# Batch 2 loaded apart from q, batch 1 in two steps, and the output's copies, PSUM buffers and DMAs regrouped

## The chip, the cores and the metric

One core of a Trainium2 chip. Its engines are TensorE (PE; PEld are its weight loads), VectorE (DVE), ScalarE (ACT), GpSimd (POOL) and SyncE (SP), which issues every DMA of this kernel. Each engine runs its own instructions in the order in which they are written; semaphores hold them together. SP's DMAs go through one queue, spread over 16 DMA engines, and are served in the order of issue. The metric is the device time of one execution in microseconds; smaller is better.

## The reference

Linear attention without a softmax, RMS norm, and a soft mixture of experts, all in float32:

```python
kv = np.einsum('bhsd,bhse->bhde', k, v)            # 8 batches, 8 heads, 576 tokens, 64
out = np.einsum('bhsd,bhde->bhse', q, kv)
out = out / sqrt(mean(out**2, -1) + 1e-6) * g_norm
x = out.transpose(0, 2, 1, 3).reshape(4608, 512)
logits = x @ phi                                   # 32 slots: 8 experts x 4
d = softmax of logits over the 4608 tokens         # one column per slot
slot_out[e] = relu((d.T @ x)[e] @ w1[e]) @ w2[e]   # 512 -> 1024 -> 512
c = softmax of logits over the 32 slots            # one row per token
return c @ slot_out                                # 4608 x 512
```

## The kernel before

The host packs the inputs into long rows, so that each DMA is one block of 128 partitions; words of 4 bytes are counted in columns (4608 columns of 128 partitions are 2304 KB). Nearly all of SBUF is one tile, `arena`, in which k and v (`kv`), q, the expert weights and at last the outputs follow one another; `KV_AT`, `Q_AT`, `W_AT` and `OUT_AT` give the places in units of 256 columns. A load into a place therefore waits until its earlier content has been read.

The work is in two stages.

Stage 1 runs over 36 tiles of 128 tokens, `for T in range(NT - 2)` and two more behind it. Tiles 0 to 8 belong to batches 0 and 1, tiles 9 to 17 to batches 2 and 3, and so on; tile 4 of each nine is half of either batch. Before a batch's first tile its matrix kv must stand in `bd`. That is done in three steps, `kv_step(b, i)`: step 0 multiplies half of k with v (`products(0)`, `products(1)`, PSUM tile kvp_kv), step 1 the other half and the last 64 tokens (`products(2)`, `products(3)`, `borders`, and ScalarE's copy to kvT), step 2 transposes kvT, multiplies it with phi (`slots`) and has ScalarE copy both to `bd`. The table `kv_steps` says ahead of which tile a step stands: for batches 2 to 7 one step ahead of each of three tiles, the first of them three tiles before the batch's own first; for batch 1, steps 0 and 1 ahead of tile 2 and step 2 ahead of tile 3. Each tile then takes four matmuls of 192 columns (eight on tile 4), `o`: attention output and logits together. ScalarE squares it and copies it out of PSUM (`sq`, `part`, `xall`), VectorE and GpSimd norm it, and in groups of six tiles the softmax over tokens and `d.T @ x` (`pS`) are kept up.

Loads for stage 1 stand at the start of SP's order; the row for batch 2 has the first 2048 columns of batch 2 and 3's q behind it. `loads_behind` puts weight loads behind tiles 9, 18, 25 and 27. That behind tile 25 (`w1` of experts 2 and 3) goes to places 0 to 32, where kv of batches 3 and 6 was, so it waits for batch 6's `borders`.

Stage 2 computes the experts: `expert_h` (ph, relu, h) and `expert_y`, which accumulates slot_out in PSUM tile `pY`, in halves of 256 columns (`hf`). w2 of experts 2 to 7 comes by halves: the load of units 5 and 6 feeds `expert_y(2..5, 1)`, the last load, unit 7, feeds `expert_y(6, 1)` and `expert_y(7, 1)`. `gather` copies a half of pY to SBUF (`y`), `mix` sums four partial results by one matmul (`pz`) and copies the sum (`z`), and `output(hf, k, f)` makes one of 12 chunks of the result: two groups `v` of two matmuls each go to a PSUM buffer `po`, ScalarE copies group 0 to the arena, VectorE group 1. The tag "m" has three such buffers for ph, pz and po. `OUT_ROWS` says which chunks leave together in one DMA. Chunks 0 to 5 are of half 0, 6 to 11 of half 1. Chunks 3 to 5 stand between the expert_y of half 1, so that PE has work while half 0 goes out.

Lines used below: L84 and L113 are load_row and load_w, L193 `products`, L208 `borders`, L217 kvT, L222 and L224 `slots`, L261 and L252 `o`, L640 expert_y, L656 `y`, L660 and L662 `pz` and `z`, L673 `po`, L681 and L683 its copies by ScalarE and VectorE, L687 the output's DMA.

Of the kernel before, what the change touches and what calls it, by code (L numbers as in the profile page):

```python
# [8 lines left out]
F32 = mybir.dt.float32  # L9
# [5 lines left out]
P = 128  # L15
# [15 lines left out]
TOK = 4608  # L31
# [4 lines left out]
KV_AT = (0, 36, 54, 0, 90, 126, 18, 54)  # L36
Q_AT = (18, 72, 108, 36)
# [12 lines left out]
    (("w2", 5, None), ("w2", 6, None)),  # L50
    (("w2", 7, None),),
)
OUT_AT = (32, 38, 44, 50, 104, 110, 116, 122, 128, 134, 140, 146)
OUT_ROWS = ((0, 1), (2, 3), (4, 5), (6, 7, 8), (9, 10, 11))
HEAD = 144
SCRATCH = 1024
EPS_RMS = 1e-6
# [5 lines left out]


@with_exitstack
def soft_moe_linear_attention(ctx: ExitStack, tc: tile.TileContext, first_in, kv_in, q0_in, kv2_in, kv4_in, kv5_in, t3_in, w_in, out):


    nc = tc.nc
# [10 lines left out]
    def place(at, n):  # L80
        return arena[:, HEAD + at * KB : HEAD + at * KB + n]

    def load_row(at, src):
        nc.sync.dma_start(place(at, src.shape[-1]), src)  # L84
# [30 lines left out]
    def w_block(kind, u, i):  # L115
        parts = homes(kind, u)
        n = UNIT // len(parts)
        k, at = divmod(i * 256, n)
        return parts[k][:, at : at + 256]
# [5 lines left out]
    load_row(KV_AT[1], kv_in[1, :, :2304])  # L125
    load_row(KV_AT[1] + 9, kv_in[1, :, 2304:])
    load_row(Q_AT[0] + 8, q0_in[:, 2048:])
    load_row(KV_AT[2], kv2_in)


    loads_behind = {
# [18 lines left out]
    sel = const.tile([P, 4, NS], F32, name="sel")  # L150
# [22 lines left out]
    ps = psA.enter_context(tc.tile_pool(name="psA", bufs=1, space=bass.MemoryType.PSUM))  # L173
# [248 lines left out]
    first = {b: 9 * (b // 2) + 4 * (b % 2) for b in range(B)}  # L422
    kvs = {}
    kv_steps = {(b, i - 3): (i,) for b in range(2, B) for i in range(3)}
    kv_steps.update({(1, -2): (0, 1), (1, -1): (2,)})

    def kv_step(b, i):
        if i == 0:
# [18 lines left out]
    def fill(n, cols=256, home=None):  # L447

        if not n:
            return  # L450
        t = home if home is not None else ps.tile([P, 2, 512], F32, tag="o", name="fill", bufs=2)[:, 1]
        for i in range(n):
            nc.tensor.matmul(  # L453
                t[:, :cols].rearrange("p (a n) -> p a n", n=256),
                lhsT=zeros[:, :P],
                rhs=zeros.unsqueeze(1).to_broadcast([P, cols // 256, 256]),
                start=True,
                stop=True,
            )
# [3 lines left out]
    for g in range(2):  # L463
        kv = Kv(0, "o" if g else "kv", 2 if g else None)
# [2 lines left out]
        kv.borders((g,))  # L467
        kv.slots((g,))
        fill(EARLY[1 + g], cols=512)
    load_row(KV_AT[3], kv_in[2])  # L470
    load_row(Q_AT[1] + 8, kv4_in)
    load_row(Q_AT[2], kv5_in)
    T_at, diag_at, pb_at, d_at, sums_at = {}, {}, {}, {}, {}
# [111 lines left out]
    ps = ctx.enter_context(tc.tile_pool(name="psB", bufs=3, space=bass.MemoryType.PSUM, reuse_waits="tile"))  # L585
# [24 lines left out]
    pY = ps.tile([P, 2, 512], F32, tag="y", name="pY", bufs=1)  # L610

    def w2_unit(e, hf):
        first = NE - LATE
        if e < first:
            return e, 8 * hf
        return first + hf * LATE // 2 + (e - first) // 2, 8 * (e % 2)
# [19 lines left out]
    def expert_y(e, hf, cs=range(8)):  # L636
        u, at = w2_unit(e, hf)
        for c in cs:
            j = c % 4
            nc.tensor.matmul(  # L640
                pY[32 * j : 32 * j + 32, hf, :256],
                lhsT=hTs[e][:, c],
                rhs=w_block("w2", u, at + c),
                start=e == 0 and c < 4,
                stop=e == NE - 1 and c >= 4,
            )
# [3 lines left out]
    zs = {}  # L650

    ys = {}

    def gather(hf):
        ys[hf] = wk.tile([P, 256], F32, tag="part", name=f"y{hf}", bufs=3)
        nc.vector.tensor_copy(out=ys[hf], in_=pY[:, hf, :256])  # L656

    def mix(hf):
        pz = ps.tile([P, 2, 512], F32, tag="m", name=f"pz{hf}")[:, 0, :256]
        nc.tensor.matmul(pz, lhsT=sel.rearrange("p a n -> p (a n)"), rhs=ys[hf], start=True, stop=True)  # L660
        zs[hf] = wk.tile([P, 256], F32, tag="part", name=f"z{hf}", bufs=3)
        nc.vector.tensor_copy(out=zs[hf], in_=pz)  # L662

    def output(hf, k, f):
        z = zs[hf]
        n = (hf * NCH + k) * 2 + f
        at = OUT_AT[n]
        st = place(at, 4 * CT * NS).rearrange("p (a n) -> p a n", a=4)
        for v in range(2):
            po = ps.tile([P, 2, 512], F32, tag="m", name=f"po{hf}_{k}_{f}_{v}")  # L670
            for u in range(2):
                lo = 32 * (2 * v + u)
                nc.tensor.matmul(  # L673
                    po[:, u, : CT * NS].rearrange("p (g x) -> p g x", g=2),
                    lhsT=z[lo : lo + 32, f * P : (f + 1) * P],
                    rhs=cT[k][lo : lo + 32],
                    start=True,
                    stop=True,
                )
            if v == 0:  # L680
                nc.scalar.copy(st[:, 0:2], po[:, :, : CT * NS])  # L681
            else:
                nc.vector.tensor_copy(out=st[:, 2:4], in_=po[:, :, : CT * NS])  # L683
        for row in OUT_ROWS:
            if row[-1] == n:
                lo, m = row[0] * 4 * CT * NS, len(row) * 4 * CT * NS
                nc.sync.dma_start(  # L687
                    out[:, lo * P : (lo + m) * P].rearrange("o (p n) -> (o p) n", p=P), place(OUT_AT[row[0]], m)
                )
# [22 lines left out]
    for e in range(4, NE):  # L712
        expert_y(e, 0)
    chunks = [(k, f) for k in range(NCH) for f in range(2)]
    gather(0)
    mix(0)
    output(0, *chunks[0])
    output(0, *chunks[1])
    output(0, *chunks[2])
    expert_y(2, 1)  # L720
    expert_y(3, 1)
    output(0, *chunks[3])
    expert_y(4, 1)
    expert_y(5, 1)
    output(0, *chunks[4])
    output(0, *chunks[5])
    expert_y(6, 1)
    expert_y(7, 1)
    gather(1)
    mix(1)  # L730
    for k, f in chunks:
        output(1, k, f)


def build_program():
    import concourse.bacc as bacc

    nc = bacc.Bacc("TRN2", target_bir_lowering=False, num_devices=1, dynamic_dma_scratch_size=SCRATCH)
    shapes = {
        "first": (P, HEAD + 2304), "kv": (3, P, TOK), "q0": (P, TOK), "kv2": (P, TOK + 2048),  # L740
        "kv4": (P, 2560 + TOK), "kv5": (P, 2 * TOK), "t3": (P, 3 * TOK),
        "w": (1, 2 * NE * P * UNIT),
    }
    args = [nc.dram_tensor(f"in_{n}_dram", s, F32, kind="ExternalInput").ap() for n, s in shapes.items()]
    args.append(nc.dram_tensor("out_0_dram", (1, 4 * NCH * P * 4 * CT * NS), F32, kind="ExternalOutput").ap())
    with tile.TileContext(nc, schedule_with_timeline_sim=True) as tc, tc.manual_schedule():
        soft_moe_linear_attention(tc, *args)
    return nc
# [58 lines left out]
```

## Time and profile before

| | us |
|---|---|
| median of 3 runs | 177.11 (176.96 to 177.36) |
| the profiled execution's own time | 177.06 |
| its span in the profile | 175.3 |
| PE busy | 149.8 (85%) |
| VectorE busy | 87.2 (50%) |
| ScalarE busy | 87.1 (50%) |
| GpSimd busy | 57.1 (33%) |
| DMA | 71.67 MB, mean 409 GB/s |

The span runs from the first to the last instruction; 1.76 us of the execution lie outside it. PE is pipelined, so its 85% is no sign of its peak. Of the chain that ended last, 49% is PE and 27% DMA. A landing is an issue's time plus the time to landing; the queue holds loads for tens of microseconds, so a long time to landing is mostly waiting behind others. One matmul in float32 makes two records, so "x8" is four matmuls.

### The profile page before, as it was taken

To read this page: it belongs to the slowest core of one execution; us is meant where nothing else is said; L and a number is where in the kernel's file an instruction comes from. 1 tells how busy PE (TensorE), PEld (TensorE's weight loads), DVE (VectorE), ACT (ScalarE), POOL (GpSimd) and SP (SyncE) were. 2 spreads that over 40 slices of the span, in tenths; PEclk is the share of its full clock that TensorE was granted. 3 is DMA by queue.
4 is the path that set the end of the run, shared out by engine and by line. 5 is a ranking of instruction groups with operands and counts; after the bars stand their busy time and mean duration, and the time that the engine had idled before them with its cause. 6 is when DMAs were issued, how large, how long until landed. Compare 5 with 4: busy or idle time off the path is not lost.

```text
span 175.3 us, 4642 instructions
## 1 busy us (share of the span) xinstructions
PE 149.8 (85%) x1977; PEld 108.6 (62%) x1977; DVE 87.2 (50%) x184; ACT 87.1 (50%) x224; POOL 57.1 (33%) x68
## 2 busy tenths in 40 slices
PE   7676798989999899999999989889999868978500
PEld 2365787979878888898897776446655533433200
DVE  1122007476567267674726797625887044446600
ACT  2026178598784886887859863103222032505500
POOL 6000063828466625576672589100000000000000
PEclk9999699999999999999999999999999999999955
DMA  5999999999999999988999999998999999996996
GB/s 201 410 436 425 449 444 410 456 431 390 463 496 425 397 404 433 426 372 292 423 456 423 421 458 436 430 439 357 471 421 408 449 415 394 410 423 286 404 404 269
DMA packets 3476, 71.67 MB, mean 409 GB/s; under 512 B 384, under 2 KB 384, under 8 KB 384
## 3 DMA queue, kind: packets, MB, share of 16 engines
q1 hardware_dynamic: 3456, 71.38, 96.0%
q8 instruction: 15, 0.25, 0.6%
q14 instruction: 5, 0.04, 0.1%
HBM read 61.94 MB, written 9.44 MB: 407 GB/s over the span
## 4 chain that ended last, share of the span: by engine, by line
PE 49%; DMA 27%; ACT 7%; DVE 5%; issue 3%; SPq 2%; POOL 1%; POOLq 1%; DVEq 0%
PE o L261 19%; DMA arena<-in_kv_dram 15%; DMA arena<-in_w_dram 12%; PE kvp_kv L193 7%; PE pY L640 4%; PE po L673 4%; PE ph L622 4%; PE pS L410 3%; PE o L252 2%; DVE arena L683 2%; SPq L84 1%; ACT sq L271 1%; PE kvp_kv L208 1%; ACT xall L279 1%; ACT bd L228 1%
## 5 line engine op out<-in xcount | busy, mean ns | idle before, releaser
L261 PE MATMUL o<-bd,arena 128*128 128x192 f32 x256 | 50.5, 341 | 1.7 <-ACT bd L238 1.1
L261 PEld LDWEIGHTS o<-bd,arena 128*128 128x128 f32 x256 | 41.9, 194 | 5.1 <-ACT bd L238 1.6
L284 DVE TENSOR_REDUCE ms<-sq 128x16 f32<-128x1024 f32 (+1 forms) x19 | 22.1, 1162 | 29.4 <-ACT sq L271 29.1
L333 POOL TENSOR_TENSOR part<-part,r 128x512 f32<-128x512 f32 x17 | 17.8, 1048 | 52.0 <-DVE r L302 52.0
L311 POOL TENSOR_TENSOR xall<-xall,r 128x512 f32<-128x512 f32 x34 | 34.7, 1042 | 0.0
L271 ACT ACTIVATE sq<-o 128x512 f32<-128x512 f32 x36 | 21.5, 598 | 11.6 <-PE o L261 11.2
L193 PE MATMUL kvp_kv<-arena 128*64 128x64 f32 x480 | 17.5, 226 | 4.2 <-DMA arena<-in_kv_dram 3.1
L279 ACT COPY xall<-o 128x512 f32<-128x512 f32 x34 | 20.7, 607 | 0.0
L193 PEld LDWEIGHTS kvp_kv<-arena 128*64 128x64 f32 x480 | 15.4, 139 | 7.8 <-DMA arena<-in_kv_dram 3.5
L681 ACT COPY arena<-po 128x768 f32<-128x768 f32 x12 | 9.3, 800 | 21.4 <-PE po L673 21.3
L346 DVE TENSOR_REDUCE logits<-part 128x64 f32<-128x512 f32 (+1 forms) x18 | 17.8, 990 | 0.0
L640 PE MATMUL pY<-arena,xall 128*32 128x256 f32 x256 | 15.2, 380 | 1.3 <-DMA arena<-in_w_dram 1.3
L683 DVE COPY arena<-po 128x768 f32<-128x768 f32 x12 | 11.2, 955 | 9.8 <-PE po L673 9.8
L673 PE MATMUL po<-logits,z 32*128 32x384 f32 x96 | 13.3, 524 | 2.3 <-DVE z L662 1.2
L640 PEld LDWEIGHTS pY<-arena,xall 128*32 128x32 f32 x256 | 8.3, 110 | 7.9 <-issue 2.2
L622 PE MATMUL ph<-arena,sTe 128*32 128x256 f32 x224 | 12.7, 380 | 0.3 <-DVE sTe L569 0.3
L278 ACT COPY part<-o 128x256 f32<-128x256 f32 x34 | 12.6, 370 | 0.0
L410 PE MATMUL pS<-xall,d 128*32 128x129 f32 x288 | 10.8, 277 | 1.2 <-ACT d L398 1.1
L673 PEld LDWEIGHTS po<-logits,z 32*128 32x128 f32 x96 | 6.0, 183 | 8.8 <-ACT arena L681 3.9
L622 PEld LDWEIGHTS ph<-arena,sTe 128*32 128x32 f32 x224 | 7.2, 110 | 5.3 <-DVE sTe L569 0.7
L453 PE MATMUL fill<-zeros 128*128 128x512 bf16 x30 | 9.1, 456 | 1.1 <-DVE zeros L145 1.1
L410 PEld LDWEIGHTS pS<-xall,d 128*32 128x32 f32 x288 | 7.2, 109 | 4.4 <-issue 3.9
(93 smaller groups left out, 137.8 us busy)
## 6 DMA issues: line engine op xcount, KB each, us to landing
arena<-in_w_dram SPq DMA_DIRECT2D x4, 4096.0 KB, 18.7
arena<-in_w_dram SPq DMA_DIRECT2D x1, 7168.0 KB, 26.5
arena<-in_t_dram SPq DMA_DIRECT2D x1, 6912.0 KB, 34.0
arena<-in_w_dram SPq DMA_DIRECT2D x1, 5120.0 KB, 17.6
arena<-in_kv_dram SPq DMA_DIRECT2D x1, 4608.0 KB, 43.0
out_dram<-arena SPq DMA_DIRECT2D x3, 1536.0 KB, 8.5
out_dram<-arena SPq DMA_DIRECT2D x2, 2304.0 KB, 7.8
arena<-in_kv_dram SPq DMA_DIRECT2D x1, 3584.0 KB, 32.6
```

The costliest lines, as they stand in the source:

```text
L193: nc.tensor.matmul(self.pkv[lo : lo + 64, w, g], lhsT=main[:, w, 1, c, lo : lo + 64], rhs=main[:, w, 0, c, lo : lo + 64], start=c == 0 and ...
L261: nc.tensor.matmul(o[:, r, :192], lhsT=q_main(2 * g + i)[:, r, at : at + P], rhs=bds[i][:, r], start=True, stop=True)
L271: nc.scalar.activation(sqs[s][:, T - starts[s]], o[:, :, 32:160], AF.Square, scale=0.125)
L279: nc.scalar.copy(xts[T % NX][:, :, :128], o[:, :, 32:160])
L284: nc.vector.tensor_reduce(out=mss[s], in_=sqs.pop(s).rearrange("p t j (w d) -> p (t j w) d", w=2), axis=AX.X, op=ALU.add)
L311: nc.gpsimd.tensor_tensor(out=x, in0=x, in1=r[:, i].rearrange("p (j w) -> p j w", w=2).unsqueeze(3).to_broadcast([P, 4, 2, D]), op=ALU.mult,)
L333: engine.tensor_tensor(out=part, in0=part, in1=rs_of[s].unsqueeze(3).to_broadcast([P, STAGES[s], H, NS]), op=ALU.mult)
L346: nc.vector.tensor_reduce(out=L[:, pos(starts[s]) : pos(starts[s]) + STAGES[s]], in_=parts.pop(s).rearrange("p t h n -> p t n h"), axis=AX ...
L410: nc.tensor.matmul(pS[32 * j : 32 * j + 32], lhsT=ds[G][:, i], rhs=x[:, j], start=i == 0, stop=i == GROUPS[G] - 1)
L622: nc.tensor.matmul(ph[32 * j : 32 * j + 32], lhsT=sTe[:, (4 * e + c) * NS : (4 * e + c + 1) * NS], rhs=w_block("w1", e, 4 * c + j), start= ...
L640: nc.tensor.matmul(pY[32 * j : 32 * j + 32, hf, :256], lhsT=hTs[e][:, c], rhs=w_block("w2", u, at + c), start=e == 0 and c < 4, stop=e == ...
L673: nc.tensor.matmul(po[:, u, : CT * NS].rearrange("p (g x) -> p g x", g=2), lhsT=z[lo : lo + 32, f * P : (f + 1) * P], rhs=cT[k][lo : lo + 32],
```

## The change

Five edits, in three places.

1. Batch 2 comes by a load of its own (4608 columns); the first 2048 columns of q for batches 2 and 3 (`q1`) come by another behind it. The host packs accordingly.
2. `kv_steps` of batch 1: step 1 moves from ahead of tile 2 to ahead of tile 3, together with step 2.
3. `copy_halves`: y is copied as two halves of 128 columns, by VectorE and by ScalarE. `mix` makes two matmuls of 128 columns, into two PSUM banks, and its sum z is copied in the same halves.
4. In half 1 every fourth group takes its PSUM buffer from tag "y", the place of pY, so that four buffers take turns. In half 0 three remain.
5. Outputs leave by four DMAs of three chunks (2304 KB each) in place of three of two and two of three; chunks 3 to 11 move in the arena. expert_y(6, 1) stands ahead of chunk 5, no longer behind it.

```diff
-OUT_AT = (32, 38, 44, 50, 104, 110, 116, 122, 128, 134, 140, 146)
-OUT_ROWS = ((0, 1), (2, 3), (4, 5), (6, 7, 8), (9, 10, 11))
+OUT_AT = (32, 38, 44, 104, 110, 116, 122, 128, 134, 140, 146, 152)
+OUT_ROWS = ((0, 1, 2), (3, 4, 5), (6, 7, 8), (9, 10, 11))
...
-    load_row(KV_AT[2], kv2_in)
+    load_row(KV_AT[2], kv_in[2])
+    load_row(Q_AT[1], q1_in)
...
-    kv_steps.update({(1, -2): (0, 1), (1, -1): (2,)})
+    kv_steps.update({(1, -2): (0,), (1, -1): (1, 2)})
...
-    load_row(KV_AT[3], kv_in[2])
+    load_row(KV_AT[3], kv_in[3])
...
+    def copy_halves(dst, src):
+        nc.vector.tensor_copy(out=dst[:, :P], in_=src[:, :P])
+        nc.scalar.copy(dst[:, P:], src[:, P:])
+
...
-        nc.vector.tensor_copy(out=ys[hf], in_=pY[:, hf, :256])
+        copy_halves(ys[hf], pY[:, hf, :256])
...
-        pz = ps.tile([P, 2, 512], F32, tag="m", name=f"pz{hf}")[:, 0, :256]
-        nc.tensor.matmul(pz, lhsT=sel.rearrange("p a n -> p (a n)"), rhs=ys[hf], start=True, stop=True)
+        pz = ps.tile([P, 2, 512], F32, tag="m", name=f"pz{hf}")[:, :, :P]
+        for f in range(2):
+            nc.tensor.matmul(
+                pz[:, f], lhsT=sel.rearrange("p a n -> p (a n)"), rhs=ys[hf][:, f * P : f * P + P], start=True, stop=True
+            )
         zs[hf] = wk.tile([P, 256], F32, tag="part", name=f"z{hf}", bufs=3)
-        nc.vector.tensor_copy(out=zs[hf], in_=pz)
+        nc.vector.tensor_copy(out=zs[hf][:, :P], in_=pz[:, 0])
+        nc.scalar.copy(zs[hf][:, P:], pz[:, 1])
...
-            po = ps.tile([P, 2, 512], F32, tag="m", name=f"po{hf}_{k}_{f}_{v}")
+            fourth = hf == 1 and (2 * n + v) % 4 == 3
+            po = ps.tile(
+                [P, 2, 512], F32, tag="y" if fourth else "m", name=f"po{hf}_{k}_{f}_{v}", bufs=1 if fourth else None
+            )
...
     output(0, *chunks[4])
+    expert_y(6, 1)
     output(0, *chunks[5])
-    expert_y(6, 1)
     expert_y(7, 1)
```

PE around batch 1's steps, before (o1, o2, o3 are tiles 1 to 3, kvp1 is batch 1):

```order
L261 MATMUL o1_187<-bd0_92,arena_63 128x192 x4
L193 MATMUL kvp1_kv_197<-arena_63 64x64 x32
L208 MATMUL kvp1_kv_197<-arena_63 64x64 x8
L261 MATMUL o2_240<-bd0_92,arena_63 128x192 x4
L222 MATMUL kvp1_kv_197<-ident_73,kvT1_0_238 128x128 x2
L224 MATMUL kvp1_kv_197<-gphi_88,kvT1_0_238 128x128 x2
L261 MATMUL o3_269<-bd0_92,arena_63 128x192 x4
```

And PE there in the changed kernel:

```order
L262 MATMUL o1_188<-bd0_93,arena_63 128x192 x4
L194 MATMUL kvp1_kv_198<-arena_63 64x64 x16
L262 MATMUL o2_215<-bd0_93,arena_63 128x192 x4
L194 MATMUL kvp1_kv_198<-arena_63 64x64 x16
L209 MATMUL kvp1_kv_198<-arena_63 64x64 x8
L223 MATMUL kvp1_kv_198<-ident_74,kvT1_0_260 128x128 x2
L225 MATMUL kvp1_kv_198<-gphi_89,kvT1_0_260 128x128 x2
L262 MATMUL o3_270<-bd0_93,arena_63 128x192 x4
```

Tile 2 moved between the two halves of batch 1's products, so that the transposes follow the borders directly.

PE behind chunk 3, before (po0_2_0 is chunk 4, po0_2_1 chunk 5, pY x16 two expert_y, pz1 the mix of half 1):

```order
L640 MATMUL pY_1426<-arena_63,xall_64 32x256 x16
L673 MATMUL po0_2_0_0_1780<-logits_97,z0_1712 128x384 x2
L673 MATMUL po0_2_0_1_1784<-logits_97,z0_1712 128x384 x2
L673 MATMUL po0_2_1_0_1788<-logits_97,z0_1712 128x384 x2
L673 MATMUL po0_2_1_1_1792<-logits_97,z0_1712 128x384 x2
L640 MATMUL pY_1426<-arena_63,xall_64 32x256 x16
L660 MATMUL pz1_1815<-y1_1813,sel_86 128x256
```

And there in the changed kernel:

```order
L641 MATMUL pY_1427<-arena_63,xall_64 32x256 x16
L685 MATMUL po0_2_0_0_1783<-logits_98,z0_1715 128x384 x2
L685 MATMUL po0_2_0_1_1787<-logits_98,z0_1715 128x384 x2
L641 MATMUL pY_1427<-arena_63,xall_64 32x256 x8
L685 MATMUL po0_2_1_0_1799<-logits_98,z0_1715 128x384 x2
L685 MATMUL po0_2_1_1_1803<-logits_98,z0_1715 128x384 x2
L641 MATMUL pY_1427<-arena_63,xall_64 32x256 x8
L666 MATMUL pz1_1819<-y1_1816,sel_87 128x128 x2
```

One expert_y of eight matmuls moved ahead of chunk 5, and pz became two matmuls.

ScalarE at the start of half 1 in the changed kernel, with the semaphores that each instruction waits for (before, the first and the last of these follow each other):

```order
L693 COPY arena<-po_2_1_0_1799 128x768 [waits PE_49]
L657 COPY y_1816<-pY 128x128 [waits DVE_49]
L671 COPY z_1822<-pz_1819 128x128 [waits DVE_49]
L693 COPY arena<-po_0_0_0_1825 128x768 [waits PE_49]
L693 COPY arena<-po_0_1_0_1833 128x768 [waits PE_49]
```

Two copies came to ScalarE, and each waits for VectorE, whose copy of the other half stands ahead of it.

## Rows read from the trace of the kernel before

**Rows 1.** The page, 40 equal slices of the span, in tenths: granted clock, DMA busy.

```profile
PEclk9999699999999999999999999999999999999955
DMA  5999999999999999988999999998999999996996
```

**Rows 2.** Chain of waits, in order of time: start us, us, what.

```profile
3.80 25.44 DMA arena<-in_kv_dram
...
29.28 1.15 PE kvp_kv L193 x32
...
146.36 1.93 PE pY L640 x32
```

**Rows 3.** Timeline of SP, single issues: start us, us, engine line op out<-in.

```profile
60.16 0.33 SPq L113 DMA_DIRECT2D arena<-in_w_dram  x1
...
79.04 0.33 SPq L113 DMA_DIRECT2D arena<-in_w_dram  x1
...
83.32 0.33 SPq L113 DMA_DIRECT2D arena<-in_w_dram  x1
...
128.25 0.33 SPq L113 DMA_DIRECT2D arena<-in_w_dram  x1
...
154.74 0.33 SPq L687 DMA_DIRECT2D out_dram<-arena  x1
162.05 0.33 SPq L687 DMA_DIRECT2D out_dram<-arena  x1
165.83 0.33 SPq L687 DMA_DIRECT2D out_dram<-arena  x1
```

**Rows 4.** DMA issues, same order without 154.74: KB each, us from issue to landing.

```profile
arena<-in_w_dram SPq DMA_DIRECT2D x1, 4096.0 KB, 20.3
arena<-in_w_dram SPq DMA_DIRECT2D x1, 4096.0 KB, 13.3
arena<-in_w_dram SPq DMA_DIRECT2D x1, 7168.0 KB, 26.5
...
arena<-in_w_dram SPq DMA_DIRECT2D x1, 2048.0 KB, 23.2
...
out_dram<-arena SPq DMA_DIRECT2D x1, 2304.0 KB, 6.9
out_dram<-arena SPq DMA_DIRECT2D x1, 2304.0 KB, 8.6
```

**Rows 5.** Windows: us, busy us of five engines, then PEclk, DMA share, GB/s.

```profile
20.00:22.00 2.00, 2.00 (x21) 1.88 (x18) 0.52 (x3) 0.80 (x3) 0.00 (x0) 0.50 1.05 450
...
78.00:80.00 2.00, 2.00 (x48) 1.86 (x43) 0.48 (x4) 1.72 (x6) 1.28 (x2) 1.00 0.25 102
...
161.00:162.00 1.00, 0.84 (x8) 0.36 (x8) 0.97 (x2) 0.17 (x1) 0.00 (x0) 1.00 0.26 111
```

**Rows 6.** Waits of SP in 60 to 90: us in total, times, longest.

```profile
SPq L113 <- PE kvp_kv L208: 8.2, 1, 8.2
```

**Rows 7.** Timeline of PE in 14.5 to 30; in brackets idle before, and releaser.

```profile
18.45 1.34 PE L193 MATMUL kvp_kv<-arena 128*64 128x64 f32 x32 [2.51 <-DMA arena<-in_kv_dram]
...
20.36 2.68 PE L261 MATMUL o<-bd,arena 128*128 128x192 f32 x8
...
27.16 1.57 PE L261 MATMUL o<-bd,arena 128*128 128x192 f32 x8
```

**Rows 8.** Timeline of all engines in 150 to 166.

```profile
152.75 0.92 PE L673 MATMUL po<-logits,z 32*128 32x384 f32 x4 [0.25 <-ACT arena L681]
...
155.60 0.42 DVE L656 COPY y<-pY 128x256 f32<-128x256 f32 x1 [0.93 <-PE pY L640]
...
157.39 1.56 PE L673 MATMUL po<-logits,z 32*128 32x384 f32 x12 [0.61 <-DVE z L662]
...
160.15 1.82 DVE L683 COPY arena<-po 128x768 f32<-128x768 f32 x2 [0.80 <-PE po L673]
```

**Rows 9.** Groups by form: count, busy us, mean ns, idle before.

```profile
L217 ACT COPY kvT<-kvp_o 128x128 f32<-128x128 f32 x1 | 0.3, 265 | 1.3 <-PE kvp_o L208 1.3
```

More of the change, by code (lines that the diff above doesn't have):

```diff
@@ L65, in soft_moe_linear_attention @@
 @with_exitstack
-def soft_moe_linear_attention(ctx: ExitStack, tc: tile.TileContext, first_in, kv_in, q0_in, kv2_in, kv4_in, kv5_in, t3_in, w_in, out):
+def soft_moe_linear_attention(ctx: ExitStack, tc: tile.TileContext, first_in, kv_in, q0_in, q1_in, kv4_in, kv5_in, t3_in, w_in, out):
     nc = tc.nc
@@ L739, in build_program @@
     shapes = {
-        "first": (P, HEAD + 2304), "kv": (3, P, TOK), "q0": (P, TOK), "kv2": (P, TOK + 2048),
+        "first": (P, HEAD + 2304), "kv": (4, P, TOK), "q0": (P, TOK), "q1": (P, 2048),
         "kv4": (P, 2560 + TOK), "kv5": (P, 2 * TOK), "t3": (P, 3 * TOK),
@@ L788 @@
         "in_first_dram": first,
-        "in_kv_dram": np.stack([kv[0], kv[1], kv[3]]),
+        "in_kv_dram": kv[:4],
         "in_q0_dram": qm[0],
-        "in_kv2_dram": np.concatenate([kv[2], qm[1][:, :2048]], axis=1),
+        "in_q1_dram": np.ascontiguousarray(qm[1][:, :2048]),
         "in_kv4_dram": np.concatenate([qm[1][:, 2048:], kv[4]], axis=1),
```

## The prediction

> **What bounds the kernel now.** I read the page's row of DMA busy tenths first. From the second slice to the 36th it stands at 8 or 9 [rows 1], so the one queue is nearly always at work, and its bytes cost time. So the question is where it runs empty, and who lets it. The chain of waits says where an engine waits for the queue instead: it starts with 25.44 us of loading up to 29.24, after which TensorE (PE) starts the products of batch 2, and it comes back at 146.36, where PE starts on weights that have just landed [rows 2].
>
> Next, each issue on SP with its time to landing [rows 3, 4] (landing = issue + time):
> - the load issued at 60.16 lands at 80.46;
> - the next, issued at 79.04, lands at 92.34; the 7168 KB issued at 83.32 land at 109.82;
> - the last weights, issued at 128.25, land at 151.45;
> - the last two outputs, issued at 162.05 and 165.83, land at 168.95 and 174.43, which ends the kernel (span 175.3, execution 177.06, median 177.11: I sum against 177.06, and the 0.05 between the two is nothing here).
>
> The last output gives the queue's speed with no gap: 2304 KB in 174.43 - 168.95 = 5.48 us, 430 GB/s. The rate test then finds the gaps. From 80.46 to 109.82 come 4096 + 7168 KB, 11.53 MB, 26.8 us at 430 GB/s, but they take 29.36: 2.5 us lost. The windows agree: the DMA share is 0.25 in 78 to 80 [rows 5]. The load of 79.04 was simply issued late, and what SP waited for last, for 8.2 us, is PE's kvp_kv on L208 [rows 6] (the borders of batch 6, whose memory the load overwrites). A second gap: the share is 0.26 in 161 to 162 [rows 5]. From 151.45 to 174.43 are 22.98 us, and the outputs, 9.44 MB, need 21.92: 1.06 lost.
>
> Everything between 29.28 and 79.04 on PE is its own and ScalarE's work; no load is waited for there. So PE's lateness at 29.28 is handed on to the issue at 79.04, and the queue's first gap is the echo of PE's wait for batch 2.
>
> **The change part by part.**
>
> Batch 2 apart from q. 6656 columns become 4608, then 2048: 1024 KB less ahead of batch 2, 1.049 MB at 430 GB/s = 2.44 us. Batch 2 lands at 29.24 - 2.44 = 26.80. The bytes stay, and the added issue on SP costs nothing, since the queue is still busy with the loads ahead of it. q of batch 2 lands at 29.24 as now and is needed only from tile 9 on, three tiles behind batch 2's first products. One wait is new: with one DMA more, a later load (in_kv5) shares a semaphore with q of batch 0 and waits for that, which tile 0 has used by then; behind it in SP stands only in_t3, which waits for tile 8 anyhow.
>
> Batch 1's second half behind tile 2. Alone, the first edit gains only if PE is ready at 26.80. [...] From 18.45 to tile 5's end at 27.16 + 1.57 = 28.73 are 10.28 us now; without tile 2, 7.60, so PE would be through at 26.05. What tile 2 covered comes back: the transposes behind the borders now wait bare for the kvT copy, 265 ns for half its width [rows 9], so I take 0.4, and 0.2 for the two hand-overs: 26.65. If the clock stays at its upper level, the other matmuls of that stretch shrink too: 1.34 for the 32 records at 18.45 were 1.15 at 29.28 [rows 2, 7], a seventh, and the slots behind them run wholly in the low stretch; I take 0.5, which makes 26.15. In both cases PE is there before 26.80, with a margin of 0.15 to 0.65. PE then starts batch 2 at about 26.84 instead of 29.28: 2.44 earlier. ScalarE evicts tile 2 earlier and has nothing new.
>
> What that is worth. The issue of 79.04 comes at 76.60. The load ahead of it lands at 80.46, unmoved, so the queue goes on without the gap. Bounds of the gain: 0 (another gap opens instead) to 2.5 us (all that the rates miss); up to 92.34 alone the loss is 92.34 - 80.46 - 9.75 = 2.1. I take 2.4, near the upper end, as the loss had reached 2.5 by 109.82 and the later issues move by 2.44 as well. The last weights then land at 151.45 - 2.4 = 149.05, those that PE waits for at 146.36 come at 143.9, and PE's work ahead of them has moved by the same 2.4.
>
> The tail. At 430 GB/s the outputs need 21.92 us from 149.05 on: 170.97, if the queue never empties. Three issues decide that, and each must come about 1.4 us before the queue is through (the output of 162.05 lands after 6.9 us, 5.48 of them transfer [rows 3, 4]).
> - Chunks 3 to 5: chunks 0 to 2 occupy the queue to 149.05 + 5.48 = 154.53; the issue must come by 153.1. Now chunk 5 is out at 154.74 [rows 3]. PE stands before chunk 5's second group until ScalarE frees a PSUM buffer: idle 0.25 ahead of 152.75, and four records in 0.92, where twelve in a row take 1.56, so four 0.52 [rows 8]. expert_y(6) fills that stall, so chunk 5 ends about where it does now: 154.74 - 2.4 = 152.35. Margin 0.75.
> - Chunks 6 to 8: the last pY now ends just before 155.60; without the stall 0.5 to 0.95 earlier, I take 0.8. From there to the first po are now 1.79 us (155.60 to 157.39) [rows 8]. Halves: VectorE takes 0.42 for 256 columns and 1.82 for two copies of 768 [rows 8], which is 0.49 for 512 more columns, so about 0.30 for 128, an estimate; ScalarE takes 0.265 for 128x128 [rows 9]. By the order's waits ScalarE's half starts behind VectorE's, so y costs 0.30 + 0.05 + 0.27 = 0.62 and not 0.42; but the first half of pz runs meanwhile, and the first po needs only VectorE's half of z. Bounds: 1.3 (all beside each other) to 2.0 (all in a row); I take 1.55, nearer to the middle. With four buffers VectorE copies without pause, 1.82 us for two [rows 8], so three chunks are out 1.0 (the first chunk's eight records of the twelve in 1.56) + 3 x 0.91 = 3.75 after the first po, now 4.66 (157.39 to 162.05). Issue at 155.60 - 0.8 - 2.4 + 1.55 + 3.75 = 157.7; needed by 154.53 + 5.48 - 1.4 = 158.6. Margin 0.9.
> - Chunks 9 to 11: another 2.73 later, 160.4; needed by 164.1.
>
> So the copies and buffers, some 3 us at the last copy, reach the end only as the 1.06 us of the second gap: the queue takes the rest.
>
> [...]
>
> [...]
>
> **Sum.** 2.4 (first gap) + 1.06 (second gap) = 3.46. The last landing comes at 170.97, the execution at 177.06 - 3.46 = 173.6 us.
>
> **The rivals.**
> 1. The clock falls again. New short idle stretches (about 0.95 before 18.45, 0.6 at the transposes) might still drop it. For: it fell after the 2.51 us [rows 5, 7]. Against: the new stretches are shorter. In the page's clock row one slice of 4.38 us stands at 6 among nines [rows 1], so it was low for some 3.5 us (0.4 / 0.5 x 4.38), which costs up to 1.75; against the margin of 0.65 PE reaches batch 2 up to 1.1 late, and I let the first gap keep half of that: 174.2.
> 2. The second gap stays: grouping by three leaves the queue waiting for chunk 5, or the y and z path is in a row and slower. For: now chunks 2 and 3 go out by themselves, and after the change nothing is issued between chunk 2 and chunk 5. Price 1:1 beyond the margin of 0.75: 174.7.
> 3. The first gap does not turn into time: the queue's later loads are held by something else and the gap opens elsewhere. For: two of the later issues also wait for PE. Against: the two later ones shown are issued 23 us and more before they land [rows 4]. Only the tail's 1.06 is left: 176.0.
> 4. Slower: PE is late for batch 2. With the clock low from 18.45 through tile 5, the 7.4 us behind 18.45 become up to 14, PE starts batch 2 at 31.5 or later instead of 29.28, the issue of 79.04 moves back with it and the first gap grows 1:1. It decides from 1.4 us on (the tail's gain and the noise). At 31.5: 177.06 + 2.2 - 1.06 = 178.2. Against: now it came back after some 3.5 us with the same work running.
> 5. No change: the pieces above cancel: 177.0.
>
> **How the numbers follow.** Forecast 0.70, the rivals 0.11, 0.08, 0.04, 0.04, 0.03. Faster: 0.70 + 0.11 + 0.08 + 0.04 = 0.93, which I lower to 0.91 for what I may not see; same 0.04, slower 0.05 (the bound is 0.2%, 0.35 us, about what a measurement can tell from no change). The forecast's own range is 173.2 to 174.2 (first gap 2.0 to 2.5, margins missed by up to 0.3); with rivals 1 and 2, 172.9 to 175.0.
>
> **What would show it.** PE's kvp_kv after tile 5 starts at 26.8, still behind its load; the clock stays at 1.00 in 18 to 24; the issue of 79.04 stands at 76.6 and the share in 76 to 80 near 1; the last weights land at 149; outputs are issued at about 146 (then queued), 152.4, 157.7 and 160.4, and the four outputs land 5.5 us apart. Wrong would be: a share well under 1 between 149 and 170, a clock of 0.50 around 20, or a last weight landing still at 151.

## The result and the profile after

The changed kernel takes 175.5 us (median of six runs, 174.35 to 176.05) against 177.17 for the kernel before; the ratio is 0.990, with a 95% interval of 0.986 to 0.994. It is faster, by 1.67 us and not by the 3.5 that were forecast, and it lies above the forecast's range. The profiled execution took 176.02 us, with a span of 174.2. Here and below a time is the median of all runs of a kernel, and a ratio leaves out the runs in which the chip was in its slower state.

The page's two rows of clock and DMA, in 40 slices of the span, answer to [rows 1]:

```profile
PEclk9969999999999999999999999999999879999955
DMA  5999999999999999999999999999999997969996
```

In the DMA row the 8s of slices 18 and 19 (the first gap) and the 6 of slice 37 (the second) have become 9s. But slices 34 and 36 now stand at 7 and 6, and the clock row shows an 8 and a 7 in slices 32 and 33, where nothing was before. (The clock's 6 in slice 5, around 20 us, has gone; the new 6 in slice 3 is 32 records at 9.29 that took 1.98 us and not 1.15.)

The front first. TensorE's timeline in 14 to 31 answers to [rows 7], with the start, the us, and in brackets the idle time before and who ended it:

```profile
17.09 1.57 PE L262 MATMUL o<-bd,arena 128*128 128x192 f32 x8
18.59 1.15 PE L194 MATMUL kvp_kv<-arena 128*64 128x64 f32 x32
...
26.79 1.15 PE L194 MATMUL kvp_kv<-arena 128*64 128x64 f32 x32 [0.78 <-DMA arena<-in_kv_dram]
```

and the window of the first gap, to [rows 5] (the share in a window counts the packets that start in it):

```profile
78.00:80.00 2.00, 2.00 (x28) 1.77 (x28) 1.23 (x2) 1.81 (x5) 1.29 (x2) 1.00 1.27 492
```

Tile 2 stands ahead of batch 1's second half, 32 records take 1.15 and not 1.34 us, tile 2's eight take 1.57 and not 2.68, with the granted clock at 1.00 in 18 to 24 for 0.50 in 20 to 22, and batch 2 starts at 26.79 for the 29.28 of [rows 2]. Then the single issues on SP (start, us) and, in the second fence, the landings of the same weight loads (KB, us from issue to landing), which answer to [rows 3, 4]:

```profile
76.55 0.33 SPq L113 DMA_DIRECT2D arena<-in_w_dram  x1
80.83 0.33 SPq L113 DMA_DIRECT2D arena<-in_w_dram  x1
...
125.76 0.33 SPq L113 DMA_DIRECT2D arena<-in_w_dram  x1
148.22 0.35 SPq L699 DMA_DIRECT2D out_dram<-arena  x1
155.40 0.34 SPq L699 DMA_DIRECT2D out_dram<-arena  x1
160.96 0.33 SPq L699 DMA_DIRECT2D out_dram<-arena  x1
163.80 0.33 SPq L699 DMA_DIRECT2D out_dram<-arena  x1
```

```profile
arena<-in_w_dram SPq DMA_DIRECT2D x1, 4096.0 KB, 14.7
arena<-in_w_dram SPq DMA_DIRECT2D x1, 7168.0 KB, 28.9
...
arena<-in_w_dram SPq DMA_DIRECT2D x1, 2048.0 KB, 25.3
...
out_dram<-arena SPq DMA_DIRECT2D x1, 2304.0 KB, 9.6
```

Read issue and landing together. Each load is issued 2.49 us earlier than before, and each takes 1.4 to 2.4 us longer to land: the first lands at 91.25 (before 92.34), the next at 109.73 (109.82), the last weights at 125.76 + 25.3 = 151.06 (before 151.45). The last output lands at 163.80 + 9.6 = 173.40, for 174.43.

TensorE, which is 2.49 us earlier through the whole middle, reaches the weights w2 3 and 4 early and waits. Its timeline there, before and after, and the windows after (PEclk, DMA share and GB/s are the last three columns):

```profile
136.75 3.66 PE L640 MATMUL pY<-arena,xall 128*32 128x256 f32 x64 [0.68 <-DMA arena<-in_w_dram]
```

```profile
136.57 5.35 PE L641 MATMUL pY<-arena,xall 128*32 128x256 f32 x64 [3.00 <-DMA arena<-in_w_dram]
```

```profile
138.00:140.00 2.00, 2.00 (x24) 1.22 (x20) 0.00 (x0) 0.00 (x0) 0.00 (x0) 0.50 1.03 442
...
147.00:148.00 1.00, 1.00 (x20) 0.59 (x24) 1.00 (x2) 0.34 (x1) 0.00 (x0) 1.00 0.42 180
148.00:149.00 1.00, 1.00 (x20) 0.49 (x16) 0.15 (x1) 0.00 (x0) 0.00 (x0) 1.00 0.49 197
154.00:155.00 1.00, 1.00 (x20) 0.42 (x16) 0.62 (x1) 0.69 (x1) 0.00 (x0) 1.00 0.44 184
```

After 3.00 us of idling the granted clock is lower (0.50 in 138 to 140, 1.00 in the other windows here), and the 64 records take 5.35 us and not 3.66. The window of 147 to 149 is the one to study: the last weights land only at 151.06, no output has been issued before 148.22, and yet the queue's share is 0.42 and 0.49. So by then, as I read the share, more than half of the 16 DMA engines are through with the last load, and some are still 2 us and more from its end. The trace holds 16 counts for each load, which come apart in time; I take them for one from each engine, an inference, as a count does not name its engine. Of the 16 counts of the last weights the first comes at 146.86, the tenth at 148.55 and the last at 151.04, beside the landing of 151.06.

### The profile page after: what moved, and what is told of

Read it like the earlier page. It is cut to its first block, busy times and chain, and to the rows that moved or that the text cites. A ratio compares the mean times of both kernels' runs of the same rounds, so it can differ in the third digit from the quotient of the medians.

```text
span 174.2 us, 4651 instructions
## 1 busy us (share of the span) xinstructions
PE 149.3 (86%) x1981; PEld 108.9 (63%) x1981; DVE 86.7 (50%) x184; ACT 88.3 (51%) x228; POOL 57.2 (33%) x68
## 4 chain that ended last, share of the span: by engine, by line
PE 50%; DMA 24%; ACT 7%; DVE 5%; issue 3%; SPq 2%; POOL 1%; POOLq 1%; DVEq 0%
PE o L262 19%; DMA arena<-in_kv_dram 13%; DMA arena<-in_w_dram 11%; PE kvp_kv L194 7%; PE pY L641 6%; PE po L685 5%; PE pS L411 3%; PE ph L623 2%; PE o L253 2%; DVE arena L695 2%; SPq L84 1%; ACT sq L272 1%; PE kvp_kv L209 1%; ACT xall L280 1%; ACT bd L229 1%
## 5 line engine op out<-in xcount | busy, mean ns | idle before, releaser
L262 PE MATMUL o<-bd,arena 128*128 128x192 f32 x256 | 49.3, 336 | 1.9 <-ACT bd L239 1.1
L262 PEld LDWEIGHTS o<-bd,arena 128*128 128x128 f32 x256 | 40.8, 190 | 5.1 <-ACT bd L239 1.6
L272 ACT ACTIVATE sq<-o 128x512 f32<-128x512 f32 x36 | 21.5, 598 | 10.2 <-PE o L262 9.8
L641 PE MATMUL pY<-arena,xall 128*32 128x256 f32 x256 | 17.1, 412 | 3.0 <-DMA arena<-in_w_dram 3.0
L194 PE MATMUL kvp_kv<-arena 128*64 128x64 f32 x480 | 17.3, 225 | 2.0 <-DMA arena<-in_first_dram 1.2
L641 PEld LDWEIGHTS pY<-arena,xall 128*32 128x32 f32 x256 | 9.1, 118 | 10.7 <-issue 6.8
L685 PE MATMUL po<-logits,z 32*128 32x384 f32 x96 | 11.5, 524 | 1.3 <-DVE z L670 0.8
L685 PEld LDWEIGHTS po<-logits,z 32*128 32x128 f32 x96 | 5.5, 183 | 5.8 <-ACT arena L693 2.5
```

What stands on the lines that cost most here:

```text
L194: nc.tensor.matmul(self.pkv[lo : lo + 64, w, g], lhsT=main[:, w, 1, c, lo : lo + 64], rhs=main[:, w, 0, c, lo : lo + 64], start=c == 0 and ...
L262: nc.tensor.matmul(o[:, r, :192], lhsT=q_main(2 * g + i)[:, r, at : at + P], rhs=bds[i][:, r], start=True, stop=True)
L272: nc.scalar.activation(sqs[s][:, T - starts[s]], o[:, :, 32:160], AF.Square, scale=0.125)
L641: nc.tensor.matmul(pY[32 * j : 32 * j + 32, hf, :256], lhsT=hTs[e][:, c], rhs=w_block("w2", u, at + c), start=e == 0 and c < 4, stop=e == ...
L685: nc.tensor.matmul(po[:, u, : CT * NS].rearrange("p (g x) -> p g x", g=2), lhsT=z[lo : lo + 32, f * P : (f + 1) * P], rhs=cT[k][lo : lo + 32],
```

## The experiments

Three theories stood after this. The fallen clock: TensorE's 3 idle us lower the clock, the outputs come late, and the front's gain goes there. The last DMA engine: a load has landed only when the last of its 16 DMA engines is through (151.04 and 151.06 above); that engine runs behind the others, had no gap before, and so gained nothing when the gap closed. The forecast: each us of a gap that closes is a us at the end. The experiments' "before" took 177.2 us in each of the three groups of runs (177.24, 177.26, 177.22).

**The change once more, and with cover for the clock.** The first has no edit; the second makes the last group of fill matmuls 14 long, so that TensorE is busy while it waits.

```
-LATE_FILL = (16, 3, 3, 1, 1, 4)
+LATE_FILL = (16, 3, 3, 1, 1, 14)
```

> The changed kernel once more, beside the three others. Theory A (the clock): PE, 2.5 us earlier, idles 3.0 us for the weights of units 3 and 4, the granted clock falls to 0.50 behind that and the 64 records of pY take 5.35 us in place of 3.66; the outputs start 1.7 late. Theory B (the last DMA engine): closing the queue's first gap moves most DMA engines but not the last one, and a load has landed only with the last, so the landings from 136 on stay within 0.5 us of before. Both: 174.3 to 176.1, profile as after. Rival C (the forecast, and one disturbed run): 173.6, weights landing at 149.

> The changed kernel with 14 in place of 4 filling matmuls ahead of the wait for units 3 and 4, so that PE is busy through most of it. Theory A: clock 1.00 from 130 to 165, pY 3.66, first output issued at 146.5 in place of 148.2, execution 0.5 to 1.7 us less than the changed kernel's slower runs: 174.3 to 175.2, and its runs lie closer together. Theory B alone (the landing binds, the clock costs nothing): same as e1 within 0.3. Landings of the weights as in e1 under both.

Measured: 175.03 us (ratio 0.986, 0.980 to 0.992) and 175.37 (0.987, 0.980 to 0.994). The change itself did not lower its clock in this profile, with nearly the same wait:

```profile
136.50 3.66 PE L641 MATMUL pY<-arena,xall 128*32 128x256 f32 x64 [2.81 <-DMA arena<-in_w_dram]
```

So the clock falls in some executions and not in others, and where it stays up the first output is issued at 146.46 instead of 148.22 and the last lands at 172.73. With the fills the clock is at 1.00 in 137 to 140 and pY takes 3.66; they bring no time beyond that. Between these two profiles the clock's price at the end is 173.40 - 172.73 = 0.67 us: too little for the missing 1.8.

**The front alone, the tail alone.** The front: batch 2 apart and batch 1's second half behind tile 2, on the kernel before. The tail: copies in halves, four buffers, expert_y(6) ahead of chunk 5, outputs by threes.

```
 front: - load_row(KV_AT[2], kv2_in)
        + load_row(KV_AT[2], kv_in[2]); load_row(Q_AT[1], q1_in)
        - (1, -2): (0, 1), (1, -1): (2,)
        + (1, -2): (0,), (1, -1): (1, 2)
 tail:  all other lines of the change
```

> Edits 1 and 2 alone (batch 2 apart, batch 1's second step behind tile 2), the tail as before. Theories A and B: load gap closed, but last weights at 151.0, PE idles 3 us at 133.5, clock low behind it, second half of the tail as before: 176.3 to 177.2. The forecast's own step (2.4 us for the first gap): 174.7.

> Edits 3 to 5 alone (halves, fourth buffer, threes, expert_y(6) ahead of chunk 5), the start as before. The forecast's own step (1.06 us for the second gap): 176.0. Theory B: the last engine works without a pause from 151.4 on, the same 176.0. Rival (threes leave the queue dry behind chunks 0 to 2 and eat the gain): 176.8 or more, with a share well under 1 between 154 and 158.

Measured: the front 176.61 (0.996, 0.993 to 1.000), the tail 176.19 (0.993, 0.989 to 0.997). The tail is worth 177.24 - 176.19 = 1.05 us, the forecast's 1.06. In its profile the window of the second gap in [rows 5] is filled:

```profile
161.00:162.00 1.00, 1.00 (x14) 0.45 (x8) 0.85 (x2) 0.88 (x2) 0.00 (x0) 1.00 0.87 369
```

The front is worth 0.63, not 2.4. The two add up to 1.68; the change was worth 1.67 in the first runs and 2.21 in this group, so such a sum holds to some 0.5 us. As the tail's part came out and the front's did not, the loss is in the front.

**The front with cover for the clock**, the front alone with 14 fills:

> Edits 1 and 2 alone (batch 2 apart, batch 1's second half behind tile 2), with 14 fill matmuls for 4, so that the clock has no cause to fall while TensorE waits for w2 3/4. Theory that the fallen clock ate the front's gain: 174.7 (the forecast's value for the front alone). Theory of the last DMA engine: the weights land no more than 0.5 us earlier than before, and the time is 176.2 +- 0.4, at most 0.5 under the front without the fills (176.61).

Measured: 176.67 (0.994, 0.991 to 0.997), no better than without fills, with pY at its 3.66 us. So the fallen clock is not what keeps the front's gain small. The last weights land at 126.03 + 24.3 = 150.3.

**The load behind the gap, issued later.** With 14 fills, the load of w1 2 and 3 moves one tile later, then two (with the next load).

```
-        25: lambda: load_w("w1", 2),
+        26: lambda: load_w("w1", 2),      # second kernel: 27, ahead of load_w("w1", 4)
```

> All edits with 14 fill matmuls, and the load of w1 2/3 issued one tile later, so that the queue's first gap comes back (issue near 78.7, a DMA share near 0.25 around 78 to 80). Theory of the last DMA engine (a load lands only when the last of its 16 engines is through, and that engine ran behind the others and never stood idle in the gap): the last weights land at 150 to 150.9, no later than without the gap, and the time is 175.4 +- 0.4 as with the fills alone. Rival, the forecast's own step (the gap is worth its 2.4 us at the end): the last weights land some 2 us later, near 152.3, and the time is 177.4.

> The same with the load of w1 2/3 two tiles later, together with the next one (issue near 80.8 to 82). Theory of the last DMA engine: that engine is through with the load ahead at 80.5, and data comes 1.4 us after an issue, so the gap now reaches it, by about 1.8 to 2.5 us: last weights at 152 to 153.5 and the time 177.2 to 178. So the price begins only between the two places. Rival, the forecast's own step: the price goes 1:1 from the first tile on, 4 to 5 us in all, last weights near 154.5, time near 179.7. Rival that issues do not matter at all: 175.4.

Measured: 174.81 (0.986, 0.980 to 0.991) and 176.42 (0.992, 0.988 to 0.996). The edit did not do what it was meant to. In the first kernel, SP issues at 76.81 and not near 78.7; in the second at 78.14, in an execution whose in_t load too was issued 1.33 us later (35.97 for 34.64), so against that the issue did not move at all. SP waits for TensorE's products there, whatever tile it stands behind. No gap came back, and the pair says nothing on its price. It shows something else. The two loads of w1 2 and 3, of the first and of the second kernel:

```profile
76.81 0.33 SPq L113 DMA_DIRECT2D arena<-in_w_dram  x1
arena<-in_w_dram SPq DMA_DIRECT2D x1, 4096.0 KB, 13.4
```

```profile
78.14 0.33 SPq L113 DMA_DIRECT2D arena<-in_w_dram  x1
arena<-in_w_dram SPq DMA_DIRECT2D x1, 4096.0 KB, 16.4
```

Landings at 90.2 and 94.5: 1.33 us between the issues, 4.3 between the landings, and the last weights stay apart (149.96 and 152.7). In the execution with the first fills the same load, issued at 77.92, had landed at 91.5, and the last weights at 150.0. So the last weights differ by some 2.7 us between executions of nearly the same program, and much of that is the lag of the last engine: the 16 counts of these weights come over 2.2 us with the first fills, over 3.1 in the first kernel here and over 4.5 in the second.

**One late engine, made on purpose.** With 14 fills, four transfers of one row of 32 KB stand behind the 7168 KB load, and as a control the same 128 KB as 128 rows of 1 KB.

```
+        for i in range(4):   # single rows
+            nc.sync.dma_start(out[:, i * 8192 : i * 8192 + 8192], place(W_AT["w1", 0][0], 8192)[:1])
+        nc.sync.dma_start(out[:, :32768].rearrange("o (p n) -> (o p) n", p=P), place(W_AT["w1", 0][0], 256))   # control
```

> All edits with 14 fills, and behind the load of 7168 KB four transfers of one row of 32 KB each (128 KB in all, 0.18% of the bytes; they write a part of the output that the real output overwrites later). One row goes to one DMA engine. Theory of the last DMA engine: at 430 / 16 = 26.9 GB/s a row takes 1.22 us, so if all four meet one engine it falls back by 4.9 us, the rest not at all, and every later load lands with it: the last weights 1 to 4.9 us later than the 149.96 with fills alone (the less, the less that engine was behind before), at 151 to 155, the DMA share of the windows before it below 1, and the time 176.2 to 179.5. Rival, the queue's rate over all bytes decides: 0.3 us, last weights at 150.3, time 175.4 to 175.7.

> The control: the same 128 KB at the same place, as one transfer of 128 rows of 1 KB, which all 16 engines share. Both theories: at 430 GB/s 0.3 us, with short rows at most 0.6; last weights at 150.0 to 151, time 175.1 to 176.0. A time like that of the single rows would say that the extra issues or the semaphores cost it, and not the one late engine.

Measured: 178.06 (1.005, 1.001 to 1.009) and 176.24 (0.993, 0.988 to 0.997); the control cost a little more than expected. Its 128 rows, issued at 81.50, landed after 27.5 us at 109.0, 0.3 us behind the 7168 KB ahead of them (81.12 + 27.6); the 0.6 us that its expectation allows for short rows was a guess that no run shows. The load of w2 5 and 6, in the kernel with single rows, then in the control; with the fills alone it was issued at 123.67 and took 21.5:

```profile
123.54 0.33 SPq L113 DMA_DIRECT2D arena<-in_w_dram  x1
arena<-in_w_dram SPq DMA_DIRECT2D x1, 4096.0 KB, 25.3
```

```profile
122.64 0.33 SPq L113 DMA_DIRECT2D arena<-in_w_dram  x1
arena<-in_w_dram SPq DMA_DIRECT2D x1, 4096.0 KB, 22.9
```

Landings: 148.8 with single rows, 145.5 with the control, 145.2 without either. In the trace the four rows' packets run straight behind each other, from 107.23 to 112.09, 1.22 us each, as on one engine. These 0.18% of the bytes, issued 40 us earlier, made this load 3.7 us later than the fills alone (3.3 later than the control), and the time 1.8 us longer than the control's. Of its 16 counts fifteen come from 143.0 to 145.2, and one at 148.9; TensorE, idle for 0.91 us, starts on it at 148.91. The sign that the changed kernel showed is there for 4 us and not for 2, with the clock at 1.00:

```profile
147.00:149.00 2.00, 1.09 (x14) 0.39 (x12) 1.66 (x2) 0.82 (x2) 0.00 (x0) 1.00 0.67 287
149.00:151.00 2.00, 2.00 (x36) 1.07 (x40) 0.16 (x1) 0.00 (x0) 0.00 (x0) 1.00 0.72 300
```

By these counts the share below 1, with a load under way, was that of engines that were through, beside one that was not. This shows, with a control, that one late engine delayed a later load by 3.3 us and the end by 1.8.

In the changed kernel's trace too a row is one packet: the four loads of 4096 KB are 512 packets of 32 KB, 1.215 us each at the median, and from 40 to 78 us mostly 16 packets are under way. That a packet goes through one engine is read from its rate: 16 x 26.97 GB/s are 431.5, next to the queue's 430. So the single rows, packet behind packet for 4.9 us (128 KB at 430 / 16 = 26.9 GB/s), look like four rows on one engine, and 3.7 of these are seen in the landing; that the rest is what this engine had been ahead of the last is an inference. Why all four met the same engine is not shown.

**Each half of the front alone.**

> Edit 1 alone: batch 2 is loaded apart from its q, and tile 2 still stands behind batch 1's second half. By the forecast's working TensorE waits 2.51 us at 18.45, the clock falls to 0.50 near 20, TensorE comes to batch 2 near 28.7 when its load has been in since 26.8, so the kvp_kv there waits for no load, the issue of 79.04 moves by 0.5 only, and the time stays within 0.5 of before: 176.7 to 177.3. Rival (the two edits are worth the same apart): the issue moves by 1.2 or more.

> Edit 2 alone: batch 1's second half behind tile 2, batch 2 still loaded together with its q. The load still lands at 29.2, so TensorE's kvp_kv of batch 2 waits for it until then, the issue of 79.04 stays within 0.2 of its place, the weights land as before, and the time is 176.9 to 177.4. Rival, both edits of the front bring a part each: the issue comes 1 us or more earlier and the time is at 176.8 or below.

Measured: batch 2 apart, alone, 177.59 (0.999, 0.994 to 1.003); batch 1's second half behind tile 2, alone, 178.6 (1.006, 1.003 to 1.009). In the first, the issue came at 76.82, 2.2 us earlier, not 0.5: that execution's first 32 products took 1.98 us and not 1.15, TensorE came some 2 us later to batch 1's second half, met its data there and did not wait. So the expectation's cause, the clock fallen at 20, was not put to the test. What it shows instead is the front's story again: the issue is early, but the last weights land at 126.09 + 24.5 = 150.6, only 0.9 earlier than before; TensorE idles 2.25 us for w2 3 and 4, runs their 64 records in 5.15 us at the lower clock (a 6 in slice 32 of the page's clock row), and the time stays. In the second, TensorE waits for batch 2 longer than before:

```profile
29.52 1.98 PE L193 MATMUL kvp_kv<-arena 128*64 128x64 f32 x32 [3.72 <-DMA arena<-in_kv_dram]
```

```profile
30.00:32.00 2.00, 2.00 (x32) 1.88 (x29) 0.00 (x0) 0.00 (x0) 2.00 (x3) 0.50 0.95 406
```

The clock falls and the issue goes back from 79.04 to 80.67. Five of the seven runs took 178.6 to 179.1 us and two 177.1 and 177.4, so not every execution pays. The wait had only been moved, and it now stands where all later work is behind it: the expectation was wrong, and this is the mechanism of the prediction's rival 4, in half the change.

## Why the prediction was wrong

**Right: the front's cause.** Batch 2 starts at 26.79 (forecast 26.84), the clock is 1.00 from 18 to 24, the issue stands at 76.55 (76.6), the first gap is gone. The clock of 0.50 in the kernel before ended at 22.66, so it held the borders (0.71 us, now 0.46) and tile 2, and not the slots, which stand at 22.88.

**Wrong: "What that is worth".** "The last weights then land at 151.45 - 2.4 = 149.05, those that PE waits for at 146.36 come at 143.9." They landed at 151.06 and, by 122.31 + 23.9 in the same view of issues, at 146.2. The step turned a mean over 16 engines into the time of the last. The rows already held what speaks against it: in the kernel before, the load ahead lands at 80.46, that is, its last engine is busy until about then; a load takes, by an estimate from an output in the tail, 1.4 us beside its transfer (6.9 - 5.48), so behind the issue of 79.04 an engine whose part ahead lands at 80.44 or later goes on without a pause. The last engine had next to no gap; the share of 0.25 in 78 to 80 told of the others. The first and the last of the 16 counts, from the traces, say what became of it:

| first and last count, us | before | after |
|---|---|---|
| the load ahead of the gap | 78.4, 80.5 | 78.5, 80.4 |
| w1 2 and 3, behind the gap | 90.6, 92.4 | 88.6, 91.2 |
| the 7168 KB | 107.6, 109.9 | 105.5, 109.7 |
| the last weights | 148.9, 151.5 | 146.9, 151.0 |

Behind the gap the first count comes 2.0 us earlier at each load, near the forecast's 2.4. The last comes 1.2 earlier at the first load, but 0.2 at the second and 0.4 at the end. As I read these counts, in the gap the early engines had stood until the late ones caught up; without it they keep their lead, and the spread of the 7168 KB grows from 2.3 to 4.2 us. So the rate test (2.5 us lost by 109.82) was true of this execution, but the gap was not what the last engine had lost: after the change the same load, with the gap closed, lands at 109.73.

Of the two bounds of that gain, 0 and 2.5, the value is near the lower: 0.39 in this execution, 0.47 in its repetition, up to 1.5 where the engines lag less (149.96, one tile later). Rival 3 named this outcome (176.0, chance 0.04) but with another cause.

**Not foreseen: where the earlier TensorE goes.** It is 2.49 us early for weights that are not, idles 3.00 us, and in some executions the clock falls, which moves the first output to 148.22 and leaves two holes (147 to 149, 154 to 155). The first costs nothing, as that output lands at 156.5 there and in the repetition; the second does. The prediction looked for a fallen clock only around 20.

**Right: the tail.** From y to the first po 1.51 us (1.55). VectorE's copies in half 1 follow each other with pauses of 0.15; from the first po to the output's issue it took 160.96 - 156.93 = 4.03 (3.75), to the next 2.84 (2.73). Start of y, its copy by ScalarE, the first po, and VectorE's pairs, from the timeline of all engines, answer to [rows 8]:

```profile
155.42 0.29 DVE L656 COPY y<-pY 128x128 f32<-128x128 f32 x1
155.74 0.27 ACT L657 COPY y<-pY 128x128 f32<-128x128 f32 x1 [0.63 <-DVE y L656]
...
156.93 1.57 PE L685 MATMUL po<-logits,z 32*128 32x384 f32 x16 [0.39 <-DVE z L670]
...
157.96 1.82 DVE L695 COPY arena<-po 128x768 f32<-128x768 f32 x2 [1.08 <-PE po L685]
...
159.93 1.82 DVE L695 COPY arena<-po 128x768 f32<-128x768 f32 x2 [0.15 <-PE po L685]
```

And the forecast's formula for the end, last weights plus 21.92 us of outputs, holds once the last weights stand right. Last weights, formula, measured end: the change's repetition 150.98, 172.9, 172.7; the tail alone 151.37, 173.3, 173.2; one tile later 149.96, 171.9, 171.85; two tiles later 152.7, 174.6, 174.6. The changed kernel's own profile (151.06, 173.0, 173.4), the fills' (150.0, 171.9, 172.6) and the control's (150.4, 172.3, 173.3) lose 0.4, 0.7 and 1.0; there the queue ran dry in part, with a share of 0.44 (154 to 155), 0.41 and 0.67 (153 to 155).

The account of the profiled executions: 174.43 - 173.40 = 1.03, of which 151.45 - 151.06 = 0.39 by the front and 1.06 - 0.42 = 0.64 by the tail. In the repetition, where the clock stays up: of 174.43 - 172.73 = 1.70 the front has 0.47 and the tail 1.23, the second gap and 0.17 by which the outputs ran faster than 430 GB/s.

**Open in part.** Why one engine lags, and why by another amount in each execution. One source may be the queue of instructions; this row of the changed kernel's page has packets, MB and share of the engines' time:

```profile
q8 instruction: 15, 0.25, 0.6%
```

0.6% of 16 x 174.2 us over 15 packets is 1.1 us for each. In the trace 16 packets of data are under way just before each of the eleven between 40 and 145 us, and while it runs 15 for nearly all of its time, before the change as after it. I take this for one engine that is away from the data for about 1 us each time. It would not be the only source: one packet of 32 KB at 79.67 took 2.7 us in the changed kernel, where most take 1.2, and with the load two tiles later one at 81.32 took 2.8. No experiment took the instruction packets away, so how much of the lag is theirs, and why it falls on other engines in other executions, is not shown.

## What to carry to other kernels

The DMA share is a mean over 16 engines, but here a waiting instruction saw only the last count of a load (with the single rows fifteen had come by 145.2, the last came at 148.9, and TensorE started at 148.91): before a gap is priced, compare the landing of the load ahead with the next issue plus what a load takes beside its transfer (here 1.4 us, an estimate); where the landing is not the earlier of the two, I expect no gap of the last engine to win back. This rests on one gap, for which it gives 0 and the profile 0.4 of 2.5; the experiments that were to reopen the gap did not. When a stage is made earlier, follow it to the next load that it waits for, and ask what the wait does there to the clock and to what is issued behind. Edits that belong together are to be tried together: here one half of the front alone was worth nothing and the other cost 1.4 us in the median.

## What was not expected of the hardware

- One late DMA engine held loads back for long: 128 KB issued near 82 us, which moved one packet of 1.22 us behind the other until 112.1, as on one engine, were still 3.7 us of lateness at 148.8.
- The clock fell after idle stretches of 2.25 (batch 2 apart, alone), 2.48 (the front alone), 2.51 [rows 7], 3.00 and 3.72 us, and did not after 2.27 (the tail alone, before 29.38) and 2.81 (the changed kernel's repetition).
- The first 32 records of products ran in 1.15 us in some executions and in 1.97 to 1.98 in others, here six of the eleven experiments' profiles, with no change in the code ahead of them; the end did not follow it. In those six the trace's first record of the upper clock stands at 12.8 to 17.3 us, in the others at 4.0 to 5.7; the page's clock row shows a 9 there all the same.
